# A fused attention and MLP kernel on one core: the MLP's second product by Strassen's half products, gelu in one ScalarE pass, attention started a round ahead

## Chip, core and metric

One core of a Trainium2 chip. The metric is the device time of one execution in microseconds (us); lower is better. Five engines work side by side, each through its own list of instructions in order: TensorE (PE; its weight loads are shown apart as PEld), VectorE (DVE), ScalarE (ACT), GpSimd (POOL) and SyncE (SP, here only a queue of DMAs). They wait for each other by semaphores.

## What is computed

Attention with global and local tokens (8 batches, 8 heads, 512 local and 32 global tokens, head size 64; a local token sees the 32 global ones and the local ones within 32 places), and behind it an MLP over all 4352 tokens:

```python
s_g  = scale * q_g @ concat(k_g, k_l).T            # global queries see everything
out_g = softmax(s_g) @ concat(v_g, v_l)
s_ll = where(abs(i - j) <= 32, scale * q_l @ k_l.T, -1e9)
s_l  = concat(scale * q_l @ k_g.T, s_ll)
out_l = softmax(s_l) @ concat(v_g, v_l)
x = concat(out_g, out_l)          # (4352 tokens, 512)
h = x @ w_in                      # (4352, 2048)
g = h * (1 / (1 + exp(-1.702 * h)))
return g @ w_out                  # (4352, 512), fp32
```

Matmul operands are bf16, sums fp32.

## The kernel before

One pass over the batches. The order on each engine is the order of the program text (a manual schedule); the text interleaves the attention of batch i + 1 with the MLP of batch i by hand.

**Attention.** A batch's 8 heads are two groups of four, `a` and `c` (objects of class `Quad` for batch 0, `Wide` from batch 1 on). `Tk` and `Tq` turn k and q with VectorE transposes (L509, L314), `kcopy`, `qcopy` and `ext` copy parts of them and of the global tokens beside them; these ten operations make up one group's preparation. `S(0)` and `S(1)` are the two score rounds on TensorE (L557), `X` their exponentials on ScalarE (L568, two halves a round), `M` the product with a 0/1 mask (L573, VectorE; for two rounds of batches 1 and 2 GpSimd). `U(0..2)` and `Gm` are the products with ones and with v (L583, L594), together `UG`; `R` turns the sums of `U(0)` and takes their reciprocal (sT, rT, rs; L459 to L463), `XL(0)` and `XL(1)` write the normalised rows xL (L468), `G` those of the global tokens into xG.

**MLP.** For a batch, `h_step(i, fc)` computes one of 16 tiles of the first product (four matmuls of 512 columns, L612), then ScalarE takes a Tanh of it (L619) and VectorE makes (tanh + 1) * h of that (L620), stored as bf16 in gT; the output is halved at the end. `o_mm(i, st)` adds four matmuls of 512 columns to one of four output tiles (L637), `o_out` copies a finished tile to SBUF on ScalarE (L651) and stores it with four DMAs on SyncE's queue. The second product of batch i stands in `phase_o(i)`, in four quarters `o(0)` to `o(3)`, between the attention steps of batch i + 1:

```python
a.S(1); a.X(1); a.M(1); o(0)
c.S(0); a.UG(); c.X(0); a.RXG(); c.M(0); o(1)
a2.T(); transpose_g(2 * n, 2 * n + 2); a2.ext()
c.S(1); c.X(1); c.M(1); o(2)
a2.S(0); c.UG(); a2.X(0); c.RXG(); a2.M(0); o(3)
```

`a2` is the first group of the batch after. At the end the 256 global tokens (i = 8) go through the MLP, their first product interleaved with the second product of batch 7.

**Buffers.** PSUM has eight banks: a pair of two-bank tiles (`spair`, for the score rounds) and four single banks (`pbank`) that everything else takes in turn, so a tile waits until the tile four places earlier has been read. k and q are loaded three batches deep through GpSimd's DMA queue (`load`), v two deep (`load_v`); gT is double.

Of the kernel before, what the change touches and what calls it, by code (L numbers as in the profile page):

```python
# [12 lines left out]
F32 = mybir.dt.float32  # L13
BF16 = mybir.dt.bfloat16
FP8 = mybir.dt.float8e4
AF = mybir.ActivationFunctionType
ALU = mybir.AluOpType
# [3 lines left out]
def kernel(  # L21
# [12 lines left out]
    nc = tc.nc  # L34

    B, H, Sl, D = q_l.shape
    Sg = q_g.shape[2]
    S = Sg + Sl
    n_tokens = B * S
    d_model = H * D  # L40
# [3 lines left out]
    scale = 1.0 / (D ** 0.5)  # L44
# [3 lines left out]
    FC = d_ff // 128  # L48
    TB = 512
# [6 lines left out]
    ctx.enter_context(tc.manual_schedule())  # L56
    consts = ctx.enter_context(tc.tile_pool(name="consts", bufs=1))
    wts = ctx.enter_context(tc.tile_pool(name="wts", bufs=1))
    ld = ctx.enter_context(tc.tile_pool(name="ld", bufs=3))
    att = ctx.enter_context(tc.tile_pool(name="att", bufs=2))  # L60
    moe = ctx.enter_context(tc.tile_pool(name="moe", bufs=2))
    psS = ctx.enter_context(tc.tile_pool(name="psS", bufs=1, space=bass.MemoryType.PSUM))
    psP = ctx.enter_context(tc.tile_pool(name="psP", bufs=4, space=bass.MemoryType.PSUM))

# [46 lines left out]
    def on_act(out_, in_):  # L111
        nc.scalar.activation(out_, in_, AF.Copy)
# [125 lines left out]
    def transpose_g(lo, hi, names="qk"):  # L238
        for name, dst, s in (("q", qgT, rqg), ("k", kgT, rkg)):
            if name not in names:  # L240
                continue
            nc.vector.transpose(dst[:, lo:hi, :32], s[:, lo:hi].bitcast(F32))
# [35 lines left out]
    def pbank(name):  # L278
        return psP.tile([128, 512], F32, name=name, tag="p")


    def spair():
        return [psS.tile([128, 2, 512], F32, name="s4", tag="s%d" % i) for i in range(2)]

    def bank(pair, j):
        return pair[j // 2][:, j % 2, :]

    class Quad:
# [166 lines left out]
            self.st["og"] = og  # L455

        def R(self):
            sT = att.tile([128, 16, 32], F32, name="sT")
            nc.vector.transpose(sT.rearrange("p a b -> p (a b)"), self.st[0])  # L459
            rT = att.tile([128, 16, 1], F32, name="rT")  # L460
            nc.vector.reciprocal(rT, sT[:, :, 0:1])
            rs = att.tile([128, 512], F32, name="rs")
            nc.vector.transpose(rs.rearrange("p (a b) -> p a b", a=16),  # L463
                                rT.to_broadcast([128, 16, 32]))
            self.st["rs"] = rs
# [139 lines left out]
    def width(i):  # L605
        return TB if i < B else B * Sg
# [3 lines left out]
    def h_mm(i, fc, hp, kcs):  # L610
        for kc in kcs:
            nc.tensor.matmul(hp[:, : width(i)], lhsT=w_in_c[:, fc // 4, kc, fc % 4 // 2, :, fc % 2],  # L612
                             rhs=(xL[i] if i < B else xG)[:, kc, :],
                             start=(kc == 0), stop=(kc == NKC - 1))

    def h_act(i, fc, hp):
        n = width(i)
        th = moe.tile([128, TB], F32, name="th", bufs=4)
        nc.scalar.activation(th[:, :n], hp[:, :n], AF.Tanh, scale=0.851)  # L619
        nc.vector.scalar_tensor_tensor(gTs[i][:, fc, :n], in0=th[:, :n], scalar=1.0,  # L620
                                       in1=hp[:, :n], op0=ALU.add, op1=ALU.mult)

    def h_step(i, fc):
        if fc == 0:
            gTs[i] = moe.tile([128, FC, TB], BF16, name="gT")
        hp = pbank("hp")
        h_mm(i, fc, hp, range(NKC))
        h_act(i, fc, hp)

    def o_mm(i, st, out=True):  # L630
        tci, f4 = divmod(st, 4)
        first = (i, tci) not in ops
        if first:
            ops[i, tci] = pbank("op")
        op = ops[i, tci]
        for fc in range(4 * f4, 4 * f4 + 4):
            nc.tensor.matmul(op, lhsT=gTs[i][:, fc, tci * 128 : tci * 128 + 128],  # L637
                             rhs=w_out_sb[:, fc, :], start=(first and fc == 4 * f4), stop=(fc == FC - 1))
        if f4 == 3 and out:
            o_out(i, tci, op)  # L640

    def o_out(i, tci, op):
        ob = moe.tile([128, d_model], F32, name="ob", bufs=6)
        last = i == B and tci == B // 4 - 1
        for lo, hi in ((0, 320), (320, 512)) if last else ((0, 512),):
            if last:
                op = pbank("op")
                for fc in range(FC):
                    nc.tensor.matmul(op[:, lo:hi], lhsT=gTs[i][:, fc, tci * 128 : tci * 128 + 128],  # L649
                                     rhs=w_out_sb[:, fc, lo:hi], start=(fc == 0), stop=(fc == FC - 1))  # L650
            nc.scalar.activation(ob[:, lo:hi], op[:, lo:hi], AF.Copy, scale=0.5)  # L651
            for j in range(4):
                eng = nc.scalar if last and j % 2 else nc.sync
                if i < B:
                    rows = out[i * S + Sg : (i + 1) * S, :].rearrange("(r t) m -> t r m", t=16)[4 * tci + j]
                else:
                    r = (4 * tci + j) * S
                    rows = out[r : r + Sg, :]
                eng.dma_start(out=rows[:, lo:hi], in_=ob[32 * j : 32 * j + 32, lo:hi])

    def act4(i, hf):
        f = slice(2 * hf, 2 * hf + 2)
        nc.vector.scalar_tensor_tensor(gTs[i][:, f, :], in0=th4s[i][:, f], scalar=1.0, in1=pts[i][hf],
                                       op0=ALU.add, op1=ALU.mult)

    pts, th4s = {}, {}

    a, c = Quad(0), Quad(1)

# [54 lines left out]
    a.XL(1)  # L724
    a.Gm()
    gTs[0] = moe.tile([128, FC, TB], BF16, name="gT")
    pt = pts[0] = spair()
    c.U(0)
    c.ekU(0)
    c.R()  # L730
# [11 lines left out]
            h_mm(0, fc, bank(pt, fc), (kc,))  # L742
    a.G()
    c.Gm()
    th4 = th4s[0] = early

    def tanh2(hf):
        f = slice(2 * hf, 2 * hf + 2)
        nc.scalar.activation(th4[:, f], pt[hf], AF.Tanh, scale=0.851)

    tanh2(0)
    c.G()
    act4(0, 0)
    for fc in range(4, FC):
        h_step(0, fc)
        if fc == 12:
            tanh2(1)
            act4(0, 1)
    def osteps(i, *sts):
        for tci, f4 in sts:  # L760
            o_mm(i, 4 * tci + f4)
# [67 lines left out]
    for fc in range(FC):  # L829
        if fc < 4:  # L830
            h_act(1, fc, hps[fc])
        elif fc in (4, 6):
            f = slice(fc, fc + 2)
            th, ps = early[:, fc - 4 : fc - 2], pt[1 - (fc - 4) // 2]
            nc.scalar.activation(th, ps, AF.Tanh, scale=0.851)
            nc.vector.scalar_tensor_tensor(gTs[1][:, f, :], in0=th, scalar=1.0, in1=ps,
                                           op0=ALU.add, op1=ALU.mult)
        elif fc >= 8:
            h_step(1, fc)
        if fc < 4:  # L840
            a.ext((fc,), on_act)
        if fc == 10:
            a.S(0)
            a.X(0, (0,))
        if fc == 11:
            a.X(0, (1,))
            a.M(0, nc.gpsimd)

    def phase_o(i):
        b = i + 1  # L850
        n = b + 1
        a, c = nq[b]
        if n < B:
            nq[n] = (Wide(2 * n), Wide(2 * n + 1))
            a2, c2 = nq[n]

        def o(tci):
            for f4 in range(4):
                o_mm(i, 4 * tci + f4)

        if i == 1:
            c.Tk(False)
            c.Tq(False)
        else:
            c.Tq()
            c.ext((3,))
        a.S(1)
        a.X(1)
        if i == 1:
            c.ext((0, 1, 2), on_act)  # L870
            c.kcopy(on_act)
            c.ext((3,), on_act)
            c.qcopy(on_act)
        a.M(1)
        o(0)
        c.S(0)
        a.UG()
        c.X(0)
        a.RXG()
        c.M(0)  # L880
        o(1)
        if n < B:
            a2.T()
            transpose_g(2 * n, 2 * n + 2)
            a2.ext()
        c.S(1)
        c.X(1)
        c.M(1)
        if n < B:
            o(2)  # L890
            a2.S(0)
            c.UG()
            a2.X(0)
        else:
            for f4 in range(3):
                o_mm(i, 8 + f4)
            for unit in range(3):
                c.U(unit)
            c.Gm(bank(spair(), 0))
            o_mm(i, 11)  # L900
        c.RXG()
        if n < B:
            a2.M(0)
        o(3)
        if i + 2 < B:
            load_v(i + 2)
        if i == 1:
            load_g(8, NQ)
        if i + 3 < B:
            load(i + 3)  # L910

    for i in range(1, B):
        if i > 1:
            for fc in range(FC):
                h_step(i, fc)
                if i + 1 < B:
                    if fc == 4:
                        nq[i + 1][1].Tk()
                    if fc in (3, 5, 7):
                        nq[i + 1][1].ext(((3, 5, 7).index(fc),), on_act)  # L920
        if i + 1 < B:
            phase_o(i)
    for st in range(FC):
        h_step(B, st)
        o_mm(B - 1, st)
    for st in range(4):
        o_mm(B, st)
    o_out(B, 1, None)


# [28 lines left out]
```

## Time and profile before

| | |
|---|---|
| runs | 297.85, 298.03, 299.1 us, median 298.03 |
| span of the profiled execution, first to last instruction | 296.1 us (the execution's own time beside its span is not given) |
| instructions | 8200 |
| ScalarE busy, mask products on VectorE L573 | 173.3 us; 26 of 1.06 us |
| Tanh L619, 128x512 | 120 of 0.598 us |
| product L620, 128x512 | 120 of 0.685 us |
| preparation of a group on VectorE (batch 3) | 76.74 to 79.62 us |
| last matmul ends | 292.5 us |

A row of a group reads: line, engine, operation, tiles (out<-in), shapes, count, then busy us and mean ns of one. In a timeline a row is start, duration, engine and line; "x4" says that four like instructions are merged. The mean of a matmul (379 ns at 512 columns) runs from its issue to its end; the next one is issued sooner, so the pace is read from starts.

### The profile page before, as it was taken

The numbers are of one execution on the slowest core, as the hardware profiler recorded it, in microseconds if no ns is written. First come the engines' busy times: TensorE is split into PE (matmuls) and PEld (weight loads), VectorE is DVE, ScalarE is ACT, GpSimd is POOL, SyncE is SP. The second block draws the span as 40 slices with busy tenths as digits, with TensorE's granted clock in tenths as the row PEclk, the third lists the DMA queues.
The fourth block names the chain that finished last, engine by engine and source line by source line (L and its number), as shares of the span: only waits on it lengthen the run. The fifth ranks groups of instructions, "written<-read, shape, count | busy, mean of one in ns | idle before, by whom it ended". The sixth has DMA issues, their size and how long they took to land.

```text
span 296.1 us, 8200 instructions
## 1 busy us (share of the span) xinstructions
PE 290.0 (98%) x3431; PEld 150.4 (51%) x3431; DVE 216.0 (73%) x422; ACT 173.3 (59%) x284; POOL 86.9 (29%) x136
## 2 busy tenths in 40 slices
PE   7999999999999999999999999999999999999995
PEld 7544446445454455445544455445544455455553
DVE  7678868887879878787879788787879766783220
ACT  4836867598447654776547653775547651663421
POOL 8973669639463003600081004400000000000000
PEclk9999999999999999999999999999999999999999
DMA  7999999997999214961199015901120021101123
GB/s 203 171 201 210 205 175 128 194 159 60 156 211 181 38 42 72 150 117 28 48 108 194 3 48 84 105 0 40 45 64 0 2 62 48 35 0 39 37 55 89
DMA packets 59541, 28.20 MB, mean 95 GB/s; under 512 B 47600, under 2 KB 49904, under 8 KB 59504
## 3 DMA queue, kind: packets, MB, share of 16 engines
q0 software_dynamic: 51664, 17.57, 53.2%
q1 hardware_dynamic: 7360, 9.45, 11.7%
q8 instruction: 27, 0.44, 0.7%
q10 hardware_dynamic: 480, 0.66, 0.7%
q14 instruction: 10, 0.08, 0.1%
HBM read 36.31 MB, written 8.91 MB: 153 GB/s over the span
## 4 chain that ended last, share of the span: by engine, by line
PE 89%; DVE 2%; issue 1%; ACT 1%; ACTq 0%; DVEq 0%
PE op L637 38%; PE hp L612 37%; PE s L557 5%; PE ov L583 5%; PE s L612 2%; PE op L649 1%; DVE xL L468 1%; PE og L594 1%; DVE rs L463 0%; ACT ob L651 0%; DVE sT L459 0%; DVE e L573 0%; ACT e L568 0%; PE ov L420 0%; PE ov L435 0%
## 5 line engine op out<-in xcount | busy, mean ns | idle before, releaser
L637 PE MATMUL op<-w_out_sb,gT 128*128 128x512 bf16 x528 | 121.5, 379 | 0.0
L620 DVE SCALAR_TENSOR_TENSOR gT<-th,hp 128x512 bf16<-128x512 f32 (+1 forms) x136 | 86.9, 654 | 35.8 <-ACT th L619 35.8
L612 PE MATMUL hp<-xL,w_in_sb 128*128 128x512 bf16 x480 | 105.4, 379 | 0.2 <-DVE xL L468 0.2
L619 ACT ACTIVATE th<-hp 128x512 f32<-128x512 f32 (+1 forms) x136 | 77.5, 572 | 41.4 <-PE hp L612 38.7
L612 PEld LDWEIGHTS <-w_in_sb 128*128 128x128 bf16 x576 | 56.0, 98 | 64.4 <-issue 0.4
L637 PEld LDWEIGHTS <-gT 128*128 128x128 bf16 x528 | 49.4, 98 | 55.0
L651 ACT ACTIVATE ob<-op 128x512 f32<-128x512 f32 (+2 forms) x35 | 20.4, 586 | 64.4 <-PE op L637 61.9
L568 ACT ACTIVATE e<-s 128x1016 bf16<-128x1016 f32 (+1 forms) x56 | 53.5, 1006 | 2.9 <-PE s L557 2.8
L97 POOL DMA_DIRECT2D v<-in_v_l_dram x40 | 31.0, 781 | 82.4 <-PE og L594 80.1
L573 DVE TENSOR_TENSOR e<-e,mask 128x1712 bf16<-128x1712 bf16 (+1 forms) x26 | 27.5, 1059 | 4.3 <-ACT e L568 3.7
L459 DVE STREAM_TRANSPOSE sT<-ov 128x512 f32<-128x512 f32 x15 | 10.8, 717 | 16.8 <-PE ov L583 15.2
L468 DVE TENSOR_TENSOR xL<-ov,rs 128x512 bf16<-128x512 f32 x29 | 18.7, 686 | 1.7 <-PE ov L435 0.4
L557 PEld LDWEIGHTS <-kT 32*128 32x128 bf16 x672 | 12.7, 93 | 12.3 <-issue 8.9
L509 DVE STREAM_TRANSPOSE kT<-rk 128x512 f32<-128x512 f32 x14 | 14.6, 1046 | 2.9 <-DMA rk<-in_k_l_dram 2.9
L557 PE MATMUL s<-q,kT 32*128 32x160 bf16 (+1 forms) x448 | 14.9, 246 | 0.0
L99 POOL DMA_DIRECT2D v<-in_v_g_dram x24 | 14.2, 590 | 2.0 <-DMA v<-in_v_g_dram 2.0
L463 DVE STREAM_TRANSPOSE rs<-rT 128x512 f32<-128x512 f32 x16 | 11.4, 711 | 0.6
L583 PE MATMUL ov<-e,v 128*32 128x128 bf16 (+3 forms) x624 | 11.7, 223 | 0.0
L314 DVE STREAM_TRANSPOSE q<-rq 128x512 f32<-128x512 f32 (+1 forms) x17 | 11.2, 662 | 0.0
L583 PEld LDWEIGHTS <-v 128*32 128x32 bf16 x672 | 10.5, 97 | 0.0
L612 PE MATMUL hp<-xG,w_in_sb 128*128 128x256 bf16 x64 | 9.6, 273 | 0.0
L557 PE MATMUL s<-qc,kT 32*128 32x120 bf16 (+1 forms) x224 | 8.0, 212 | 0.0
(109 smaller groups left out, 183.2 us busy)
## 6 DMA issues: line engine op xcount, KB each, us to landing
out_dram<-ob SPq DMA_DIRECT2D x132, 64.0 KB, 2.6
rq<-in_q_l_dram POOLq DMA_DIRECT2D x5, 512.0 KB, 6.9
rk<-in_k_l_dram POOLq DMA_DIRECT2D x5, 512.0 KB, 8.7
v<-in_v_l_dram POOLq DMA_DIRECT2D x24, 96.0 KB, 4.5
w_in_sb<-in_moe_w_in_dram POOLq DMA_DIRECT2D x8, 256.0 KB, 7.6
w_out_sb<-in_moe_w_out_dram POOLq DMA_DIRECT2D x4, 512.0 KB, 10.3
rq<-in_q_l_dram POOLq DMA_DIRECT2D x5, 256.0 KB, 6.5
rk<-in_k_l_dram POOLq DMA_DIRECT2D x5, 256.0 KB, 7.5
```

The costliest lines, as they stand in the source:

```text
L97: nc.gpsimd.dma_start(out=vt[0:n, hs, c, :D], in_=vs[FIRST[c] : FIRST[c] + n, hs])
L468: nc.vector.tensor_mul(self.x[:, 2 * self.u + h, :], self.st[1 + h], self.st["rs"])
L509: nc.vector.transpose(flat[:, 0:Sl].rearrange("p (r t) -> p t r", t=16), loaded[self.b][0][:, self.u].bitcast(F32))
L557: nc.tensor.matmul(bank(self.ps, j)[:, at : at + n], lhsT=self.k[p, KEYS[c] : KEYS[c] + 128, e], rhs=qs[p, :, :, e], start=(e == 0), stop= ...
L568: nc.scalar.activation(self.E[rnd][:, 2 * i : 2 * i + 2, :n], self.ps[i][:, :, :n], AF.Exp, scale=scale)
L573: eng.tensor_mul(e, e, mask[:, rnd : rnd + 1, :n].to_broadcast([128, 4, n]))
L583: nc.tensor.matmul(ov[32 * j : 32 * j + 32, :].rearrange("p (t r) -> p t r", t=16)[:, t0:t1, r0 : r0 + nr], lhsT=lv, rhs=self.E[rnd][:, j, ...
L612: nc.tensor.matmul(hp[:, : width(i)], lhsT=w_in_c[:, fc // 4, kc, fc % 4 // 2, :, fc % 2], rhs=(xL[i] if i < B else xG)[:, kc, :], start=( ...
L619: nc.scalar.activation(th[:, :n], hp[:, :n], AF.Tanh, scale=0.851)
L620: nc.vector.scalar_tensor_tensor(gTs[i][:, fc, :n], in0=th[:, :n], scalar=1.0, in1=hp[:, :n], op0=ALU.add, op1=ALU.mult)
L637: nc.tensor.matmul(op, lhsT=gTs[i][:, fc, tci * 128 : tci * 128 + 128], rhs=w_out_sb[:, fc, :], start=(first and fc == 4 * f4), stop=(fc = ...
L651: nc.scalar.activation(ob[:, lo:hi], op[:, lo:hi], AF.Copy, scale=0.5)
```

## The change

The second product of batches 2 to 7 and of the global tokens is cut into 2 x 2 x 2 blocks: the tokens of a batch into two halves, the 2048 gelu columns into even and odd tiles, the 512 outputs into two halves of 256. Strassen's seven half products take the place of eight, each of 8 matmuls of 256 columns (numbered 1 to 7, worked in the order 3, 4, 1, 6, 5, 2, 7). A `Pair` is two output tiles worked together; a batch has two (p0, p1), the global tokens one. Five sums of weight blocks are made once on VectorE (`weight_sums`), and four sums of gelu blocks per batch (`g_sums`, in four sets of four instructions, as the gelu tiles get ready). A pair takes two banks, x and y: `m3` copies half product 3 on ScalarE before 5 is added on top of it, `z` and `zm` add 4 and 1 to it on VectorE, `evict` copies x, `sub` and `add` make the four blocks, `store` sends eight DMAs on SyncE's queue. In the tail both banks are slices of one two-bank tile.

Gelu is one ScalarE activation straight from PSUM to gT, in another function table than Exp, with a dummy gelu (`gelu_table`) behind a batch's last exponentials. Tanh, the VectorE product, and the factor of 0.5 go. From batch 2 on both score rounds of the next group `a2` are worked in the phase before, so that a phase starts with `a.UG`; three of the four mask products of a phase are on GpSimd. The loads move to the head of the phase, k and q are loaded two batches deep instead of three, gT and the buffers sT and rs are single. Batch 1 keeps the plain second product, in a new order (`phase_o1`).

```diff
-    ld = ctx.enter_context(tc.tile_pool(name="ld", bufs=3))
+    ld = ctx.enter_context(tc.tile_pool(name="ld", bufs=2))
-    moe = ctx.enter_context(tc.tile_pool(name="moe", bufs=2))
+    moe = ctx.enter_context(tc.tile_pool(name="moe", bufs=1))
...
+    def gelu(out_, in_):
+        nc.scalar.activation(out_, in_, AF.Gelu_apprx_sigmoid)
     def h_act(i, fc, hp):
         n = width(i)
-        th = moe.tile([128, TB], F32, name="th", bufs=4)
-        nc.scalar.activation(th[:, :n], hp[:, :n], AF.Tanh, scale=0.851)
-        nc.vector.scalar_tensor_tensor(gTs[i][:, fc, :n], in0=th[:, :n], scalar=1.0,
-                                       in1=hp[:, :n], op0=ALU.add, op1=ALU.mult)
+        gelu(gTs[i][:, fc, :n], hp[:, :n])
...
+    class Pair:
+        def mm(self, *ks):
...
+            for k in ks:
+                lv, rv, where = {
+                    1: (s[0], wsum[0], 2), 2: (s[2][:, :, n : 2 * n], b11, 1), 3: (a11, wsum[1], 0),
+                    4: (a22, wsum[2], 1), 5: (s[2], b22, 0), 6: (s[1], wsum[3], 3), 7: (s[3], wsum[4], 2),
+                }[k]
...
+                for g in range(FC // 2):
+                    nc.tensor.matmul(out_, lhsT=lv[:, g, tt * 128 : tt * 128 + 128], rhs=rv[:, g, :],
...
+        def m3(self, eng="act"):
+            self.zz = moe.tile([128, 2, HM], F32, name="zz")
...
+                on_act(self.zz[:, 0], self.x[:, :HM])
+        def z(self):
+            nc.vector.tensor_add(self.zz[:, 0], self.zz[:, 0], self.x[:, HM:])
+        def zm(self):
+            nc.vector.tensor_add(self.zz[:, 1], self.zz[:, 0], self.y[:, :HM])
+        def evict(self):
+            self.ob = moe.tile([128, 4, HM], F32, name="ob", bufs=3)
+            on_act(self.ob[:, 1:3], self.x.rearrange("p (h m) -> p h m", h=2))
+        def sub(self):
+            nc.vector.tensor_sub(self.zz, self.zz, self.ob[:, 1:3])
+        def add(self):
+            nc.vector.tensor_add(self.ob[:, 0:4:3], self.zz, self.y.rearrange("p (h m) -> p h m", h=2))
...
+    def phase_o1():
...
+        a.X(0)
+        a.M(0, nc.gpsimd)
+        loads_after(1)
+        weight_sums(0, 1, 2, 3, 4)
+        o_parts(1, 0, 1, 2, 3, 4)
...
+        a.S(1)
+        a.X(1)
+        a.M(1)
+        o_parts(1, 5, 6)
+        c.S(0)
+        c.X(0)
+        o_parts(1, 7)
+        a.UG()
+        a.R()
+        c.M(0)
+        c.S(1)
+        c.X(1)
+        a.XL(0)
+        a.XL(1)
+        a.G()
+        c.M(1)
+        a2.T()
+        transpose_g(6, 8)
+        a2.ext()
+        o_parts(1, 8, 9, 10)
+        a2.S(0)
+        a2.X(0)
+        a2.M(0)
+        o_parts(1, 11)
+        c.UG()
+        c.RXG()
+        a2.S(1)
+        a2.X(1)
+        gelu_table()
+        a2.M(1)
+        o_parts(1, 12, 13, 14, 15)
+
+    def phase_o(i):
...
+        loads_after(i)
+        a.UG()
+        c.S(0)
+        a.R()
+        g_sums(i, 6, 8, (0,))
+        a.XL(0)
+        g_sums(i, 6, 8, (1, 2, 3))
+        p0.mm(3, 4, 1)
+        c.X(0)
+        c.M(0, nc.gpsimd)
+        p0.m3()
+        p0.z()
+        a.XL(1)
+        a.G()
+        c.S(1)
+        c.X(1)
+        p0.mm(6)
+        p0.zm()
+        c.M(1)
+        p0.mm(5, 2)
+        p0.evict()
+        p0.mm(7)
+        p0.sub()
+        p0.add()
+        p0.store()
+        c.U(0)
+        if a2:
+            a2.S(0)
+            a2.X(0)
+            a2.M(0, nc.gpsimd)
+        c.U(1)
+        c.U(2)
+        c.Gm()
+        c.RXG()
+        p1.mm(3, 4, 1, 6)
+        p1.m3()
+        p1.z()
+        p1.zm()
+        if a2:
+            a2.S(1)
+            a2.X(1)
+            a2.M(1, nc.gpsimd)
+        p1.mm(5, 2)
+        p1.evict()
+        gelu_table()
+        p1.mm(7)
+        p1.sub()
+        p1.add()
+        p1.store()
...
+                    if fc == 13 and i + 2 < B:
+                        a2 = quads_of(i + 2)[0]
+                        a2.T()
+                        transpose_g(2 * i + 4, 2 * i + 6)
+                        a2.ext()
+                if fc in (4, 8, 12):
+                    g_sums(i, fc // 2 - 2, fc // 2)
...
+    ps = [Pair(B - 1, tt, [bank(pt, 2 * tt), bank(pt, 2 * tt + 1)]) for tt in range(2)]
+    todo = [(p, k) for p in ps for k in (3, 4, 1, 6, 5, 2, 7)]
     for st in range(FC):
         h_step(B, st)
-        o_mm(B - 1, st)
-    for st in range(4):
-        o_mm(B, st)
-    o_out(B, 1, None)
+        if st < len(todo):
+            p, k = todo[st]
+            p.mm(k)
+            if k == 6:
+                p.m3()
+                p.z()
+                p.zm()
+            if k == 2:
+                p.evict()
...
+    p = Pair(B, 0, [bank(pt, 0), bank(pt, 1)])
+    p.mm(3, 4, 1, 6)
```

## The prediction

> **What bounds the kernel now.** I read the page first (busy shares, chain, groups), then TensorE's own waits, then the chain in order of time for one batch, then the timelines of the other engines.
>
> ```profile
> PE 290.0 (98%) x3431; PEld 150.4 (51%) x3431; DVE 216.0 (73%) x422; ACT 173.3 (59%) x284; POOL 86.9 (29%) x136
> ...
> PE 89%; DVE 2%; issue 1%; ACT 1%; ACTq 0%; DVEq 0%
> ...
> L637 PE MATMUL op<-w_out_sb,gT 128*128 128x512 bf16 x528 | 121.5, 379 | 0.0
> ```
>
> ```profile
> PE w L182 <- POOL ones L158: 1.1, 1, 1.1
> PE s L353 <- DVE q L314: 0.5, 1, 0.5
> PE s L336 <- ACT e L384: 0.4, 1, 0.4
> PE hp L612 <- DVE xL L468: 0.2, 1, 0.2
> ```
>
> TensorE waits 2.2 us in the whole span; from 18 to 292.5 us it is one closed stream. So work taken off it is worth its full time, and every new wait costs its full time. The chain gives prices:
>
> ```profile
> 119.10 13.81 PE hp L612 x64
> 132.91 0.56 PE s L557 x24
> 133.47 3.56 PE op L637 x16
> ...
> 265.19 0.86 PE op L637 x4
> 266.06 0.44 PE hp L612 x4
> ```
>
> A batch's first product takes 13.81 us, a score round S 0.56, a quarter of the second product 3.56. Four 512-column matmuls take 0.86 (216 ns each), four 256-column ones 0.44 (109 ns each).
>
> **What TensorE saves.** Per batch the second product is 64 x 0.216 = 13.82 us before and 7 x 16 = 112 matmuls of 256 columns after, 112 x 0.109 = 12.21: 1.61 less. Global tokens: 16 x 0.216 + 16 x (0.136 + 0.082) (the runs of 320 and 192 columns at L649) = 6.94 before, 56 x 0.109 = 6.10 after. Together 6 x 1.61 + 0.84 = 10.5 us. Could 256 columns cost more in a long run? The group's busy time per matmul is 9.6/64 = 150 ns, by which a batch would lose 3 us; but that counts the tail of each group of four, and the 16 matmuls of 192 columns ran at 82 ns each. I take 109.
>
> **Off TensorE.** Gelu in one pass: I price it as the Tanh of the same tile, 0.60 us; only above 0.86, the pace of the first product, would it count. The 136 VectorE products (86.9 us) go, but never set the pace. The five weight sums (2048 elements, about 1.2 us each) fall into batch 1's first product, where VectorE now has nothing else: nothing. A sum of gelu halves (two bf16 tiles in SBUF) isn't in the trace: 0.34 us for 512 elements by the slope of the mask products, 0.65 by the product that is removed. I take 0.34, since the mask product has the same operands; the upper end adds 1.4 us in each of four phases. The loads move to the head of the phase on GpSimd's queue, past the mask products: 11 DMAs, some 8 us of its time. It reaches them during the first product before (13.8 us; their buffers are free by its third step), so they cost nothing; late, they would put c.M(0) and with it c.U(0) off one for one. Two load buffers instead of three, and one gT instead of two, also cost nothing: a load is wanted some 20 us after its buffer is free, and the first gelu of a batch follows the last read of the gT before.
>
> **The new waits**, in the order of the changed kernel's instructions on each engine. Rows:
>
> ```profile
> 45.94 3.33 POOL L573 TENSOR_TENSOR e<-e,mask 128x1760 bf16<-128x1760 bf16 x1 [0.23 <-ACT e L568]
> ...
> 48.67 1.51 DVE L573 TENSOR_TENSOR e<-e,mask 128x1712 bf16<-128x1712 bf16 x1
> ...
> 76.74 1.04 DVE L509 STREAM_TRANSPOSE kT<-rk 128x512 f32<-128x512 f32 x1
> ...
> 79.62 1.04 DVE L573 TENSOR_TENSOR e<-e,mask 128x1712 bf16<-128x1712 bf16 x1
> ```
>
> ```profile
> 1.82 1.28 ACT L675 ACT_TABLE_LOAD   x1 [1.82 <-issue]
> ...
> 67.41 1.89 ACT L568 ACTIVATE e<-s 128x992 bf16<-128x992 f32 x2
> ```
>
> (1) *Batch 1's second product (phase_o1).* VectorE holds, in order, c.M(1) (1.0 us; it waits for c.X(1), 1.93), then ten operations that turn the next pair's k and q (2.88, 76.74 to 79.62), then nothing TensorE could skip: a2.S(0) waits for the tenth. From the end of c.S(1) that is 0.1 + 1.93 + 1.0 + 2.9 = 6.0 us, and VectorE comes about 0.9 late because a's R, c.M(0), XL and G stand in front. TensorE has three groups of four matmuls, 2.6 us, to do meanwhile: a wait of 4.2. Smaller ones: c.S(0) behind a.X(1), which starts late after a table load, an output copy and three copies on ScalarE (0.6); two Gm, whose bank is the output tile that ScalarE copies only after X (0.5 each); the first matmul of the last quarter, whose bank sT reads late (0.3). Sum 6.1; with a2.S(1) and its change of shape moved here (0.7, out of the next phase) batch 2's first product starts 7.0 later.
>
> (2) *phase_o of batches 2 to 5*, times from the end of the first product. VectorE: the third set of gelu sums starts when gelu 11 is done (-2.6) and ends at -0.9; then the ten turning operations until 1.9; only then R's sT (2.6), to rs 3.65, one sum, XL(0) 4.65. TensorE: UG and S(0) end at 2.05. Half product 3 needs the bank that sT reads: it waits until 2.7 (0.6). Half product 1 needs XL(0)'s bank: 4.45 to 4.7 (0.25). ScalarE: the load of the Exp table stands behind the wait for c.S(0), so X(0) runs from 3.45 to 5.4, in time for S(1) at 5.7. GpSimd now does three mask products per phase. The 48.67 row shows what that does to VectorE: its product with two SBUF inputs, else 1.0, took 1.51 and ended 0.9 after GpSimd's ended at 49.27; it was held. So c.M(1) (wanted at 8.3, GpSimd busy 5.9 to 9.25) ends at 10.2, and c.U(0) waits 0.3. At the end a2.M(1) on GpSimd runs 18.5 to 21.85 and holds p1.sub, wanted at 19.05; add then ends at 23.15, and the fourth tile of the next first product, whose bank add reads, waits 1.5. The phase takes 20.6 against 33.05 - 13.81 = 19.24 before: +1.36, four times +5.4. Batch 6 has no next pair: its exponentials end after S(1) is due (0.7), c.M(1) is held (0.3), p1's bank comes late (0.6); 18.3 against 18.8, -0.5.
>
> On this hold the Trainium skill, SBUF — State Buffer, section "SBUF: two separate sides", says that a VectorE operation with two SBUF inputs and a GpSimd operation that reads SBUF lock each other out for a whole instruction; the 1.51 us row agrees, and the rule speaks against this change. On the table load it goes beyond the row: its page ScalarE: Activation LUTs, section "What ACT_TABLE_LOAD costs", counts about 1.38 us of draining on top of a load of 1.28, which no row here shows; by that the time would be some 322.4.
>
> (3) *The tail.* Here both banks of a pair are slices of one tile, so waits are coarser: half product 5 waits for m3, z and zm, all after half product 6 (a delay of 0.2, then 0.38 and twice 0.42 by the 256-column Tanh and product; less the 0.44 us of first product in between: 1.0), and 7 waits for the copy of 5 and 2 (0.4). Batch 7 has this twice, 2.9. The global pair has nothing in between: 1.45 + 0.85 = 2.3. Then sub and add (0.7 each, 128x512) and eight stores on SyncE's queue alone, 0.43 apart by
>
> ```profile
> 292.94 0.85 ACTq L659 DMA_DIRECT2D out_dram<-ob  x2
> ```
>
> (two in 0.85); before, two queues issued two each after a copy of 0.33. The last matmul is followed by 6.7 us against 3.65: +3.05. Tail: -1.6 - 0.85 + 2.9 + 2.3 + 3.05 = +5.8.
>
> **The sum** against the profiled execution's span of 296.1: 7.0 + 5.4 - 0.5 + 5.8 = +17.7, a span of 313.8. Its own time outside the span isn't shown; the median of the runs is 298.03, 1.9 above the span, so 315.7. Left out: a slower TensorE clock after the 4.2 us wait. The 21 first matmuls of 128 columns took 2.42 us, twice the pace of later ones; 5 us of that would cost up to 2.6, and in the other direction nothing.
>
> **Rivals.** (A) *GpSimd gets in first.* c.M(0) on GpSimd is ready at 5.5, while the phase's last gelu sums run (4.6 to 5.9). If it starts before the last sum, that sum, then z, zm and c.M(1), come 3.3 later; half product 5 waits 2.6 for z, and the phase takes 23.0. Four times +2.4 more: 325.3. For it: the two start within 0.1 us of each other; against: the sums follow each other with no gap.
>
> (B) *No hold.* The 1.51 row is one instance; were it chance, c.M(1), p1.sub would run when ready: 1.8 less in four phases and 0.4 in batch 6: 308.1.
>
> (C) *Not slower.* Only TensorE's own work counts: VectorE loses 86.9 us and about 14 of mask products and gains some 75, so it runs ahead and its order doesn't matter. Place: a2.S(0) in batch 1 and half products 3 and 5. It decides if the waits stay below 10.5 - 3.05 = 7.5 us; with none, 298.0 - 7.5 = 290.5. For it: before, nothing on VectorE ever held TensorE in these stages. Against: before, the turning operations stood ahead of c.M(1) and a whole quarter-product (3.5 us) lay between; now a chain of 6.0 us has 2.6 of cover, whatever VectorE's total.
>
> **Chances.** Forecast 0.43, A 0.25, B 0.18, C 0.14 (0.10 faster by over 0.5%, 0.04 within 0.5%, about what a measurement of this kernel can tell from no change). Slower 0.86. The forecast's own range is 312 to 321 (the clock, and the upper price of the sums); with A and B it reaches from 305 to 327, and leaves out C and the ends of A and B.
>
> **What would show it.** TensorE's waits: one of some 4 us before a2.S(0) near 81 us, put to VectorE's copy to kT; some 0.6 us at half product 3 behind sT in batches 2 to 5 and not in 6; 1.5 at the fourth tile of a first product behind VectorE's add; 1 to 1.5 at half product 5 in the tail. VectorE: operations with two SBUF inputs that take 1.5 to 4 us beside GpSimd's mask products (long sums: A; none long: B). ScalarE: 16 table loads of 1.28. The matmuls of 256 columns should follow at 109 ns; above 120 the saving is gone and my first step is wrong. A span below 300 would mean that the order of VectorE's list is not what I read.

## The result and the profile after

316.11 us (median of 4 runs, 315.45 to 316.56) against 298.56 (297.85 to 300.35): 1.057 times as long, 95% interval 1.052 to 1.062. The profiled execution took 315.94, its span is 314.2; 313.8 was forecast for the span and 315.7 for the time.

First the page of the changed kernel: busy times, and the share of the chain by engine.

```profile
PE 284.7 (91%) x3705; PEld 181.3 (58%) x3727; DVE 203.9 (65%) x441; ACT 189.0 (60%) x301; POOL 130.4 (41%) x150
...
PE 20%; DVE 3%; ACT 2%; issue 2%; ACTq 0%; DVEq 0%
```

TensorE is busy 5.3 us less than before, in a span that is 18.1 longer. (The forecast saving was 10.5. Busy time hides part of it: some 1.6 us of the slow matmuls shown below, and at each of some 25 waits about 0.16, since the last matmul before a wait counts as busy for 273 or 379 ns where the next could have started after 109 or 216; an estimate from these rows.) The chain could be followed back through less than 30% of the span, so it says nothing of the middle; TensorE's own waits do (line, tile, releaser: us in total, times, longest).

```profile
PE hp L612 <- DVE ob L735: 5.6, 4, 1.4
PE s L557 <- DVE kT L542: 3.9, 1, 3.9
PE s L710 <- DVE zz L725: 3.3, 3, 1.4
PE px L710 <- DVE sT L459: 2.7, 6, 0.5
PE s L710 <- ACT ob L112: 1.3, 3, 0.7
...
PE s L557 <- ACT e L568: 0.5, 1, 0.5
```

Before, all waits were 2.2 us. Now these rows alone hold 17.3: the fourth tile of four first products behind `add` (L735), the round of batch 1 behind the turning operations (L542), half product 5 in the tail behind `zm` (L725), half product 3 behind sT, half product 7 behind `evict`.

Where the time lies, by the starts of the first products (batch 1 51.83 before, 52.20 after; batch 2 85.89 and 93.54; batch 7 250.78 and 262.66; span's end 296.1 and 314.2): up to batch 2 +7.7, batches 2 to 7 +4.2, tail +6.2; together 18.1. Forecast were 7.0, 4.9 and 5.8.

Batch 1's second product on TensorE, from the timeline (start, us, engine, line):

```profile
85.03 0.53 PE L557 MATMUL s<-q,kT 32*128 32x160 bf16 x16 [3.95 <-DVE kT L542]
...
85.60 1.89 PE L644 MATMUL op<-w_out_sb,gT 128*128 128x512 bf16 x4
```

The wait is 3.95 us. The four matmuls behind it took 1.89 instead of 1.04, and started 0.40 to 0.43 apart, half the usual pace; with the products of `UG` behind them (2.21 instead of 1.45) that is 1.6 us.

The end of a phase (batch 2), GpSimd's row first, then VectorE's:

```profile
126.00 3.24 POOL L573 TENSOR_TENSOR e<-e,mask 128x1712 bf16<-128x1712 bf16 x1 [2.36 <-ACT e L568]
```

```profile
126.46 3.33 DVE L732 TENSOR_TENSOR zz<-zz,ob 128x512 f32<-128x512 f32 x1 [2.62 <-ACT ob L112]
129.88 0.69 DVE L735 TENSOR_TENSOR ob<-zz,py 128x512 f32<-128x512 f32 x1
```

`sub` reads two tiles in SBUF and started while GpSimd's mask product ran: 3.33 us. `add`, right behind it, has one input in PSUM: 0.69. And the middle of the phase, VectorE's last gelu sum and GpSimd's first mask product:

```profile
112.72 0.41 DVE L687 TENSOR_TENSOR gs<-gT 128x512 bf16<-128x512 bf16 x1
...
115.53 1.70 DVE L573 TENSOR_TENSOR e<-e,mask 128x1712 bf16<-128x1712 bf16 x1 [0.46 <-ACT e L568]
```

```profile
112.92 3.40 POOL L573 TENSOR_TENSOR e<-e,mask 128x1760 bf16<-128x1760 bf16 x1 [15.15 <-ACT e L568]
```

GpSimd started only 0.2 us behind the last sum: so little kept it from getting in first. `c.M(1)`, later, was held until it was done: 1.70 instead of 1.0. The table load that decides when GpSimd starts:

```profile
109.54 1.28 ACT L568 ACT_TABLE_LOAD   x1 [1.39 <-PE s L557]
110.84 1.93 ACT L568 ACTIVATE e<-s 128x1016 bf16<-128x1016 f32 x2
```

### The profile page after: what moved, and what is told of

Read it like the earlier page. It is cut to its first block, busy times and chain, and to the rows that moved or that the text cites. A ratio compares the mean times of both kernels' runs of the same rounds, so it can differ in the third digit from the quotient of the medians.

```text
span 314.2 us, 8811 instructions
## 1 busy us (share of the span) xinstructions
PE 284.7 (91%) x3705; PEld 181.3 (58%) x3727; DVE 203.9 (65%) x441; ACT 189.0 (60%) x301; POOL 130.4 (41%) x150
## 5 line engine op out<-in xcount | busy, mean ns | idle before, releaser
L617 ACT ACTIVATE gT<-hp 128x512 bf16<-128x512 f32 x120 | 71.5, 596 | 35.2 <-PE hp L612 33.8
L573 POOL TENSOR_TENSOR e<-e,mask 128x1760 bf16<-128x1760 bf16 (+1 forms) x15 | 49.8, 3322 | 101.5 <-ACT e L568 89.3
L710 PEld LDWEIGHTS <-gs 128*128 128x128 bf16 x480 | 46.0, 98 | 10.9 <-DVE zz L725 2.5
L687 DVE TENSOR_TENSOR gs<-gT 128x512 bf16<-128x512 bf16 x72 | 28.3, 415 | 25.0 <-ACT gT L617 25.0
L732 DVE TENSOR_TENSOR zz<-zz,ob 128x512 f32<-128x512 f32 x13 | 19.6, 1511 | 19.5 <-ACT ob L112 19.5
L710 PE MATMUL py<-wsum,gs 128*128 128x256 bf16 x240 | 30.3, 273 | 0.1
L644 PE MATMUL op<-w_out_sb,gT 128*128 128x512 bf16 x122 | 29.7, 388 | 0.7 <-issue 0.3
L710 PEld LDWEIGHTS <-gT 128*128 128x128 bf16 x192 | 18.6, 97 | 5.4 <-issue 2.5
L710 PE MATMUL px<-wsum,gT 128*128 128x256 bf16 x160 | 19.1, 272 | 2.9 <-DVE sT L459 2.7
L644 PEld LDWEIGHTS <-gT 128*128 128x128 bf16 x128 | 12.0, 99 | 14.5 <-issue 0.6
L710 PE MATMUL px<-w_out_sb,gs 128*128 128x256 bf16 x160 | 19.1, 273 | 0.0
## 6 DMA issues: line engine op xcount, KB each, us to landing
w_out_sb<-in_moe_w_out_dram POOLq DMA_DIRECT2D x4, 512.0 KB, 10.5
```

Source lines behind the costliest of these rows:

```text
L573: eng.tensor_mul(e, e, mask[:, rnd : rnd + 1, :n].to_broadcast([128, 4, n]))
L617: nc.scalar.activation(out_, in_, AF.Gelu_apprx_sigmoid)
L687: nc.vector.tensor_tensor(sums[i][k][:, g, : n // 2], x[:, g], y[:, g], op)
L710: nc.tensor.matmul(out_, lhsT=lv[:, g, tt * 128 : tt * 128 + 128], rhs=rv[:, g, :], start=(g == 0 and k in (1, 3)), stop=(g == FC // 2 - 1 ...
L732: nc.vector.tensor_sub(self.zz, self.zz, self.ob[:, 1:3])
```

## Experiments

Each is one edit of the changed kernel, unless it says otherwise. The edits are shown in part (`...` marks a gap), and the comments in them are added here. Times are medians; the kernel before beside them was 299.1 to 299.2.

**1. Turning operations early.** Theory: VectorE's order makes the wait of 3.95. Rival: ScalarE's exponentials do.

```diff
         a.S(1)
         a.X(1)
+        a2.T()
+        transpose_g(6, 8)
+        a2.ext()
         a.M(1)
...
         c.M(1)
-        a2.T()
-        transpose_g(6, 8)
-        a2.ext()
```

> Batch 1's second product: the ten operations that turn the next pair's k and q stand ahead of a.M(1) on VectorE instead of behind c.M(1). Order theory: the next pair's first score round starts about 81.2 us into the span instead of 85.0 and waits for nothing; a.M(1) comes 0.9 later, which costs a.U at most 0.5. With the wait goes the stretch behind it in which 512-column matmuls take 0.43 us instead of 0.22 (1.5 us). Together 5 less than 316.1: 311 (310 to 312). If the stretch at half pace has another cause than the wait, only 3.7 less: 312.4. Rival, ScalarE's exponentials and not VectorE's list hold that round: no change, 315.5 to 316.5.

Measured: 315.0 us, ratio to before 1.053 (1.048 to 1.058), in the range of neither. The wait and the slow matmuls behind it went, and batch 2's first product starts 37.8 us after batch 1's instead of 41.3: 3.5 won, not 5. The rest went in two places, both on VectorE's timeline:

```profile
73.77 1.29 DVE L501 COPY kT<-kT 128x192 f32<-128x192 f32 x1
...
108.47 3.37 DVE L687 TENSOR_TENSOR gs<-gT 128x512 bf16<-128x512 bf16 x1
```

GpSimd ran its mask products from 71.63 to 74.95 and from 108.24 to 111.55. The copy (0.26 elsewhere) was held by the first, and `a.U` waited 1.28 for `a.M(1)` behind it. The sum was held by the second: this is rival A of the prediction, in batch 2 alone, whose phase took 1.6 longer. Why there? In the changed kernel the table load of `X(0)` stood behind the scores of c.S(0) (the row of 109.54 above). Here, in batch 2 alone, it began at 104.84, before c.S(0), which started at 105.48:

```profile
104.84 1.28 ACT L568 ACT_TABLE_LOAD   x1
```

The exponentials came 1.3 sooner relative to the phase, and so did GpSimd. `X(0)` waits for two things, TensorE's scores and the last user of its e buffer; that the moved operations exchanged which of the two waits stands ahead of the load is an explanation that no row shows. So the order theory holds for the wait, which is gone, and ScalarE falls as its cause; the expected sum failed on two more holds, which experiments 6 and 7 take up.

**2. The last mask product on VectorE.** Theory: GpSimd's product holds `sub`. Rival: chance, or its input.

```diff
-            a2.M(1, nc.gpsimd)
+            a2.M(1)
```

> In batches 2 to 5 the mask product of the next pair's second round, at the end of the phase, is on VectorE (1.0 us) instead of GpSimd (3.24 us). Hold theory: the subtraction of the second pair, 3.33 us beside GpSimd's product, takes 0.7 and ends by 127.8 instead of 129.8; the fourth tile of the next first product no longer waits (1.5): four times 1.5 less, 310 (309.5 to 311). Rival, the subtraction is long for another reason (its input, the table load on ScalarE beside it): 315.5 or more, since VectorE now has 1.0 us more to do ahead of it.

Measured: 309.65 us, ratio 1.035 (1.032 to 1.039). VectorE's timeline, same place (the mask product, 1.05 us, stands right ahead):

```profile
127.61 0.69 DVE L732 TENSOR_TENSOR zz<-zz,ob 128x512 f32<-128x512 f32 x1
```

The wait at the fourth tile is gone, and a batch takes 32.62 us instead of 34.19. 1.57 four times is 6.3 of the 6.5 us won. VectorE does more and the kernel is faster.

**3. What is held.** GpSimd's product stays; the `sub` of a batch's second pair reads PSUM. A copy of one column ahead of it keeps its start where it was.

```diff
+        def sub_psum(self):
+            nc.vector.tensor_copy(self.hop(), self.ob[:, 1, 0:1])
+            nc.vector.tensor_sub(self.zz, self.zz, self.x.rearrange("p (h m) -> p h m", h=2))
...
-        p1.sub()
+        p1.sub_psum()
```

> GpSimd's mask product stays where it is. The second pair's subtraction reads the product's bank in PSUM instead of the copy in SBUF, so that it has one SBUF input; a VectorE copy of one column of the copied tile ahead of it keeps it behind ScalarE's copy, as before, and so beside GpSimd's product. If the hold is between GpSimd and an operation with two SBUF inputs: the subtraction takes 0.7 us beside the running mask product, the fourth tile's wait of 1.5 goes, 310 (309.5 to 311.5). Rival, GpSimd's product slows or stops whatever VectorE does: the subtraction stays at 2 to 3.3 us, 314 to 316.5.

Measured: 309.63 us, ratio 1.036 (1.032 to 1.040). GpSimd and VectorE:

```profile
125.40 3.24 POOL L573 TENSOR_TENSOR e<-e,mask 128x1712 bf16<-128x1712 bf16 x1 [2.37 <-ACT e L568]
```

```profile
125.94 0.69 DVE L733 TENSOR_TENSOR zz<-zz,px 128x512 f32<-128x512 f32 x1
126.72 0.69 DVE L742 TENSOR_TENSOR ob<-zz,py 128x512 f32<-128x512 f32 x1
127.33 1.05 DVE L509 STREAM_TRANSPOSE kT<-rk 128x512 f32<-128x512 f32 x1
```

A subtraction with one input in PSUM, an addition of the same kind and a transpose ran at their usual length within GpSimd's 3.24. So GpSimd does not slow VectorE as such. The rival falls, and the same 6.5 us come back without moving any work off GpSimd.

**4. Two tiles for the tail's banks.** Theory: the tail's waits are by tile. Rival: by VectorE's and ScalarE's order.

```diff
-    ps = [Pair(B - 1, tt, [bank(pt, 2 * tt), bank(pt, 2 * tt + 1)]) for tt in range(2)]
+    ps = [Pair(B - 1, tt, [bank(pt, tt), bank(pt, 2 + tt)]) for tt in range(2)]
-    p = Pair(B, 0, [bank(pt, 0), bank(pt, 1)])
+    p = Pair(B, 0, [bank(pt, 0), bank(pt, 2)])
```

> In the tail the two banks of a pair of half products are taken from two different tiles instead of one. Theory, the waits are by tile: half product 5 then waits for z alone and not for zm (0.95, 0.95 and 1.39 become 0.5, 0.5 and 0.95), and half product 7, which writes the other tile, no longer waits for ScalarE's copy of 5 and 2 (0.25, 0.30 gone; of the last 0.73 only some 0.35 is won, since the final addition then waits for the subtraction): 2.3 less, 313.8 (313.3 to 314.5). Rival, the waits come from the order of VectorE and ScalarE: within 0.5 of 316.1.

Measured: 311.32 us, ratio 1.042 (1.038 to 1.046): 4.8 won, twice the 2.3 expected. All six waits at L710 in the tail are gone, 4.6 us. The expectation kept half product 5's wait for `z`; but `m3` too had waited by tile, for half products 1 and 6, which write the other half of it. With a tile of its own, x is copied sooner, in the global tokens' pair by two half products, and there half product 5 is under way before `zm` starts (298.71 and 298.91 us; in the changed kernel it waited 1.39 for the end of `zm`).

**5. The wait filled.** Is the half pace behind the wait of 3.95 the wait's doing?

```diff
         o_parts(1, 8, 9, 10)
+        zero(17, ops[1, 2])
```

> Seventeen 512-column matmuls of zeros onto a bank that is being accumulated are put into TensorE's wait ahead of the next pair's first score round in batch 1's second product (3.7 us of work into a wait of 3.95). The round itself can start no sooner (VectorE's tenth turning operation at 85.0). Clock theory: the matmuls behind the wait ran at half pace because TensorE had stood still; now they run at 216 ns, and batch 2's first product starts 1.5 sooner: 314.6 (314 to 315.2), and the span then shows the whole of the extra 7.1 us in phase_o1 as 5.6 of waits and moved work and 1.5 of clock. Rival, the half pace comes from something else (loads that arrive, VectorE or ScalarE beside it): 316.1 within 0.5.

Measured: 315.38 us, ratio 1.056 (1.052 to 1.060), 0.7 less, between the two ranges expected; the profile decides. The same stretch of the changed kernel and then of this one (stretch, us, busy of PE, PEld, DVE, ACT, POOL, granted clock, DMA share, GB/s):

```profile
85.00:88.00 3.00, 2.97 (x52) 1.47 (x56) 0.20 (x1) 2.23 (x3) 0.00 (x0) 0.60 0.99 142
```

```profile
85.00:88.00 3.00, 2.61 (x99) 1.87 (x101) 0.28 (x1) 2.31 (x3) 0.00 (x0) 1.00 0.97 145
```

The round started at 84.95, so the wait's end didn't move; the clock stayed at 1.00, and 99 matmuls were worked in these 3 us instead of 52. So the standing still took the clock down. Of the 1.6 us, half was not won: TensorE now arrived early at a Gm (0.39 behind an output copy) and at sT's bank (0.41).

On this the Trainium skill, TensorE: Matmul & The Clock Gate, section "What's actually happening", has the clock fall to half after an idle window of some 3.4 us; the wait of 3.95 us agrees, with a clock of 0.50 from 85.58 to 88.99 us (0.60 is the mean over the stretch shown). Experiment 6 shows falls after shorter waits, which this rule doesn't have.

**6. The exponential's table early.** A test of rival A: GpSimd is let in first.

```diff
         loads_after(i)
+        exp_table()    # a one-column Exp
         a.UG()
```

> The table of the exponential is loaded at the head of each phase of batches 2 to 6 (a one-column exponential ahead of a.UG) instead of behind c.S(0). X(0) then ends 1.1 to 1.3 sooner, and GpSimd's mask product c.M(0) starts at about 111.7 in batch 2, before VectorE's last three sums of gelu halves, as it did by chance of one wait in batch 2 of the kernel with the turning operations early (there one sum took 3.37 us and the phase 1.64 longer). Theory: an earlier exponential makes the kernel slower: one sum of 3.3 to 3.4 us in each of the five phases, half product 1 waits about 1 for it and half product 5 about 0.9 for z; four times 1.65, batch 6 about +1 (its wait for the exponentials goes): 323.7 (321.5 to 325). Rival, GpSimd and VectorE share and nothing is held that was not held before: 315.5 (batch 6 gains 0.7).

Measured: 331.6 us, ratio 1.110 (1.106 to 1.114), 15.5 slower, where 7.6 was expected. GpSimd, VectorE and TensorE:

```profile
111.58 3.32 POOL L573 TENSOR_TENSOR e<-e,mask 128x1760 bf16<-128x1760 bf16 x1 [13.86 <-ACT e L568]
```

```profile
111.75 3.44 DVE L690 TENSOR_TENSOR gs<-gT 128x512 bf16<-128x512 bf16 x1
```

```profile
151.66 0.39 PE L713 MATMUL py<-wsum,gs 128*128 128x256 bf16 x2 [1.00 <-DVE gs L690]
152.93 3.20 PE L713 MATMUL px<-w_out_sb,gs 128*128 128x256 bf16 x16 [0.87 <-DVE zz L725]
```

The mechanism is the one named, with its two waits of 1.00 and 0.87. An exponential that ends 1.3 us sooner makes the kernel 5% slower. Batch 2's phase lost 2.0, near the 1.65 expected; batches 3 to 5 lost 3.4 to 3.6 each and batch 6 2.6 (about 1 was expected), because half products 5 and 2 behind the waits took 3.20 to 3.47 instead of 1.91. The stretches around these waits, in batch 3 and then in batch 2, columns as in experiment 5:

```profile
149.95:153.36 3.41, 1.54 (x12) 0.99 (x11) 3.41 (x5) 1.87 (x2) 1.37 (x1) 1.00 0.00 0
153.36:156.77 3.41, 3.41 (x18) 2.42 (x16) 1.98 (x6) 0.60 (x1) 0.00 (x0) 0.50 0.00 0
```

```profile
112.40:115.81 3.41, 2.23 (x37) 1.35 (x36) 3.41 (x3) 1.89 (x2) 2.50 (x1) 1.00 0.00 0
115.81:119.23 3.42, 2.72 (x28) 2.26 (x27) 3.26 (x9) 0.60 (x1) 0.00 (x0) 1.00 0.00 0
```

The granted clock was 0.50 for one stretch of 3.41 us. In batches 3 to 6 such stretches begin at 153.36, 190.91, 228.45 and 266.00 us, 37.55 apart, which is eleven times 3.41: they look like steps of a fixed grid. Each comes right behind a step in which TensorE was busy for only 1.4 to 1.6 us, with both waits in it (batches 3 and 4) or a single one of 2.15 or 2.01 (batches 5 and 6). In batch 2 the same two waits lie on either side of a boundary of that grid, with 2.23 and 2.72 us busy, and the clock stayed at 1.00. What such a wait costs thus hung on where it fell; that is read from these cases, no run varied it.

**7. Batch 1 without GpSimd's holds.** Experiment 1, with two mask products on VectorE: batch 1's `a.M(0)`, and `c.M(0)` of every phase behind `zm`.

```diff
-        a.M(0, nc.gpsimd)        # phase_o1
...
         c.qcopy(nc.vector.tensor_copy)
+        a.M(0)
...
-        c.M(0, nc.gpsimd)        # phase_o
...
         p0.zm()
+        c.M(0)
         c.M(1)
```

> The turning operations early, as in the first experiment, and two of GpSimd's mask products on VectorE: a.M(0) of batch 1's second product, and c.M(0) of every phase, put ahead of c.M(1). Theory: the copy to kT that took 1.29 us in the first experiment was held by GpSimd's a.M(0), and the sum of 3.37 us in batch 2 by c.M(0). Without them the copy takes 0.26, a.U waits 0.3 instead of 1.28, the sums take 0.42 each and c.M(1) 1.0 instead of 1.70. From 315.0: 1.0 less in phase_o1, 1.65 less in batch 2, 0.3 less in each of batches 3 to 6: 311.1 (310.3 to 312). Rival, the first experiment gained little because the waits go round whatever is moved: 314 to 316.

Measured: 310.39 us, ratio 1.038 (1.035 to 1.042), as expected. The copy takes 0.26 again, no sum is long, batch 1 to batch 2 is 36.4 (34.06 before, 41.3 in the changed kernel).

**8. Turning operations at step 9.** For the wait at half product 3.

```diff
-                    if fc == 13 and i + 2 < B:
+                    if fc == 9 and i + 2 < B:
```

> One edit in the changed kernel: the operations that turn the pair after next's k and q stand at step 9 of the first product instead of step 13, ahead of the third set of gelu sums instead of behind it. Theory: VectorE reaches R's first transpose when UG's sums are there and not 0.5 to 0.8 late, so half product 3 no longer waits for sT in batches 2 to 5 (0.52) and half product 1 not for XL(0) (0.25): four times 0.5 to 0.8 less, 313.5 (312.8 to 314.2). Rival, the wait is for the transpose itself (0.7 us from the end of U(0)) and not for what stands in front of it: 316.1 within 0.5.

Measured: 315.9 us, ratio 1.056 (1.052 to 1.061): the time is the rival's, nothing won that can be measured. But the wait for sT went, as the theory had it, and another took its place three half products later:

```profile
113.36 0.28 PE L557 MATMUL s<-qc,kT 32*128 32x108 bf16 x6 [0.47 <-ACT e L568]
```

c.S(1) needs the exponentials of c.S(0) to have read their bank, and they stand behind the table load. It is the wait that the changed kernel has in batch 6 alone; now all five phases have it, 2.4 us in all. The early table would take this wait away and does harm alone (experiment 6); the next kernel has both, with `c.M(0)` off GpSimd.

**9. All mends.** Experiments 1, 2, 4, 6, 7 and 8 together, and the global tokens' stores on two queues:

```diff
-            nc.sync.dma_start(out=rows, in_=ob[32 * j : 32 * j + 32])
+            eng = nc.scalar if i == B and j % 2 else nc.sync
+            eng.dma_start(out=rows, in_=ob[32 * j : 32 * j + 32])
```

> All mends at once, with the half products and the one-pass gelu kept: turning operations of batch 1 ahead of a.M(1), those of later batches at step 9 instead of 13; all mask products but a2.M(0) (and batch 1's c.M(0)) on VectorE; the exponential's table at the head of the phase; two tiles for the two banks in the tail; the global tokens' eight stores on two queues. Theory, terms that add: phase_o1 5.7, end of phase 4 x 1.5, sT and XL(0) 4 x 0.75, c.M(1) 5 x 0.3, batch 6 1.0, tail 4.8 + 1.7; 23.7 from 316.1: 292.4 (290.5 to 295), ahead of the kernel before by some 2%. Rival, the half products' waits and the extra VectorE work are not a matter of order, and other waits take the place of these: 298 to 304, no better than before.

Measured: 293.96 us (6 runs, 293.84 to 295.72), ratio 0.985 (0.982 to 0.989). The profiled execution took 295.43.

```profile
PE 281.0 (96%) x3705; PEld 180.6 (62%) x3727; DVE 199.8 (68%) x451; ACT 189.8 (65%) x306; POOL 97.1 (33%) x140
```

```profile
PE s L353 <- DVE q L314: 1.4, 1, 1.4
...
PE op L647 <- DVE sT L459: 0.3, 1, 0.3
```

The stream is closed again, but for the opening and a few waits of 0.2 to 0.3. A batch takes 31.62 us against 33.05 before: 1.43 less, where the half products alone give 1.61. Of the 22.2 us from the changed kernel, experiments 7, 2 and 4 give 5.7, 6.5 and 4.8 one by one. The other 5 came from step 9 with the early table (0.8 a batch, though neither won anything alone), batch 6 (0.8) and the tail (1.2).

**10. A half product twice.** The mended kernel; does TensorE's work count in full?

```diff
-                for g in range(FC // 2):
+                for g in list(range(FC // 2)) * (2 if k == 6 else 1):
```

> The mended kernel (293.96) with half product 6 of every pair run twice (the output changes by that): TensorE then does 64 matmuls of 256 columns a pair, as many column passes as the plain product, 13 pairs x 8 x 109 ns = 11.3 us more. Theory: TensorE's stream is closed in the mended kernel, so all of it counts: 305.3 (304.3 to 305.8), and what the seven half products save on TensorE is worth its full time once nothing else waits. Rival, part of it hides in waits that are still there: 294 to 302.

Measured: 305.5 us, ratio 1.022 (1.019 to 1.026): 11.5 more for 11.3 of matmuls. A batch takes 33.36, 1.74 more, which is 16 x 109 ns. So doing seven half products and not eight is worth the full price of one, once the order lets it through.

**11. The global tokens by plain matmuls.** The mended kernel with the last product as before.

```diff
-    p = Pair(B, 0, [bank(pt, 0), bank(pt, 2)])
+    for tci, runs in ((0, ((0, 512),)), (1, ((0, 320), (320, 512)))):
...
+            nc.scalar.activation(ob[:, lo:hi], op[:, lo:hi], AF.Copy)
```

> The mended kernel with the global tokens' second product as plain 512-column matmuls, the last tile in runs of 320 and 192 columns with a copy and two-queue stores behind each, as in the kernel before, and no gelu sums for them. TensorE +0.84 (6.94 against 6.10), and behind the last matmul a copy of 192 columns and four stores instead of subtraction, addition and eight: 3.6 us as before instead of 6.1. Theory: 293.96 + 0.84 - 2.5 = 292.3 (291.7 to 293.2). Rival, the stores that still drain from batch 7 set the end: 294.0 to 294.8.

Measured: 292.52 us (4 runs), ratio 0.979 (0.976 to 0.982). From the last matmul's end (286.21) to the span's end (290.8) it is 4.6 us instead of 6.1; not 3.6 as before, since SyncE's queue, which sends eight of the twelve stores, is busy until 288.4. This is the fastest version: 6.7 us ahead of the kernel before.

## Why the prediction was right

The forecast was built from the order of each engine's list and the hold by GpSimd, and both were right. That the time came within 0.4 us is partly luck: up to batch 2 it cost 0.7 more than forecast, batches 2 to 7 0.7 less, the tail 0.4 more.

**TensorE's saving.** 256-column matmuls went at 109 ns (16 issued in 1.75 us), and a batch gets 1.43 of the 1.61 once mended. In the changed kernel the saving is there, beneath the waits. The prices off TensorE held too: gelu 0.596 (0.60 forecast), a weight sum 1.21 (1.2); a sum of gelu halves took 0.42, nearer to the 0.34 taken than to the 0.65 beside it.

**Step (1).** Forecast +7.0 (its terms add up to 6.8); batch 1 to batch 2 took +7.3. The main term, 4.2, was 3.95. The other terms were sized too large: c.S(0) and the last quarter did not wait, one Gm waited 0.35. What filled their place was the term left out, the clock: 1.6 us, inside the bound of 0 to 2.6 that stood beside the sum. The total is right partly because two errors cancel. The opening cost another 0.4, which no step had.

**Step (2).** Forecast 0.6, 0.25, 0.3 and 1.5 for half product 3, half product 1, c.U(0) and the fourth tile; measured 0.52, 0.2, 0.1 and 1.36. Batches 3 to 5 took 34.14 to 34.41 against 33.05, +1.1 to +1.4 where +1.36 was forecast; batch 6, without the wait that it inherits from batch 5's `add`, took 0.9 less than before (31.84 in experiment 2, where that wait is gone, against 32.71), where 0.5 was forecast. Experiments 2 and 3 show the wait of the fourth tile, and 8 those of half products 3 and 1, to be what they were said to be; that of c.U(0) was not tested by itself. Half product 3's can't be mended alone, though: behind its 0.52 stands a wait of 0.47 (experiment 8).

**Step (3).** Half product 5 waited 0.95, 0.95 and 1.39 (forecast 1.0, 1.0, 1.45), 7 waited 0.25, 0.30 and 0.73 (0.4, 0.4, 0.85), and 6.7 us follow the last matmul (6.7). Batch 7's two pairs, 1.4 each, add up to 2.8, where 2.9 was written.

**The hold.** Experiments 2 and 3 show the Trainium skill's lock (SBUF — State Buffer, "SBUF: two separate sides") here: an operation with two SBUF inputs was held (1.70 and 3.33 us in the changed kernel, 3.37 in experiment 1, 3.44 in experiment 6), the same subtraction with one input in PSUM was not (0.69). The Trainium skill's other case there, an operation in a two-port mode, would fit the copy of experiment 1 (1.29 instead of 0.26, until GpSimd was done), but no run shows in which mode that copy ran.

**The rivals.** A (the sums held) missed by 0.2 us in the changed kernel, so that the forecast came out and not A was luck as well; experiment 6 let it in, and its price was 2.0 in batch 2, where 2.4 a phase was forecast, and up to 1.6 more where the clock fell too. B (no hold) is refuted by `sub`'s 3.33 to 3.40 us in each of four phases and by experiments 2 and 3. C (only TensorE's work counts, 290.5) is refuted for this order, and experiments 9 and 10 show an order in which it comes nearly true. The longer price of the table load (322.4) is refuted by its rows: X(0) starts 1.30 us after the load, which is the load alone.

## What to carry to other kernels

- In a closed stream, work taken off the bounding engine is worth its full time, but only as far as every other engine's list still reaches each hand-over in time; walk those lists instruction by instruction, because totals of busy time (VectorE had 12 us less to do here) say nothing of it.
- GpSimd is no free engine beside VectorE: an operation of 3.3 us there lengthened VectorE's sums, subtractions and mask products with two SBUF inputs by up to 3.1 us. Here a product of 1 us was better left on VectorE (experiment 2), or the VectorE operation beside it given an operand in PSUM (experiment 3).
- Mend waits in groups: one removed alone can uncover the next (experiment 8), or start something sooner that does harm (experiment 6).

## What the runs showed of the hardware

- The granted clock fell to 0.50 for 3.41 us at a time, behind steps of 3.41 us in which TensorE was busy for 1.4 to 1.6 us (experiment 6) or 0.55 (the changed kernel, 82.17 to 85.58, around the end of the wait of 3.95). Two waits of 1.00 and 0.87 us were enough where both lay in one step (batches 3 and 4), and not where a boundary divided them (batch 2); single waits of 0.95 and 1.39 in the tail left it at 1.00. A short wait can thus cost more than its length: half products 5 and 2 took 1.3 us longer in batch 3.
- One table load of 1.28 us stood behind the scores that its exponential reads (109.54, the changed kernel) or ahead of them (104.84, experiment 1). An edit elsewhere changed that and moved the exponential by 1.3 us; why is argued only.
- VectorE transposes (1.05 us) and operations with a PSUM input (0.69) ran beside GpSimd at their usual length, and a copy of a single column took 0.15 us there (all experiment 3), while a copy of 192 fp32 columns was held (experiment 1).
